# A second stage in an upper and a lower half: where the "y" products stand in a step

## The chip, the core and the metric

The kernel runs on one core of a Trainium2 chip. The metric is device time in microseconds (us): the median of three runs is 182.15 (181.86 to 182.22).

The core's engines have their own instruction streams and meet at semaphores: TensorE (PE, matrix products into the accumulator memory, PSUM, with its weight loads shown as PEld), VectorE (DVE), ScalarE (ACT), GpSimd (POOL) and SyncE (SP), which here issues the stores. PSUM has eight banks; a bank holds one result tile of 128 rows by 384 columns of float32 here.

## The reference, cut

Two layers. The first mixes each position with the six before it, with softmax weights per head. The second keeps 64 frequencies of the sequence, mixes channels in each of them, goes back, and ends in a product with `w_ch`:

```python
    x = attn_out
    X = np.fft.rfft(x, axis=1)
...
    y = np.fft.irfft(Y, n=S, axis=1)
    u = x + y
    return (u + np.maximum(u @ w_ch, 0.0)).astype(np.float32)
```

So the output is relu(x W + y W) + y + x. Since y comes from 64 frequencies, both y and y W are products with a table of 128 rows (64 cosines, 64 sines).

## The kernel before

All work up to some 108 us is untouched by the change: the input comes in, the seven-tap mixing runs as products with a band matrix (L270), the transform to 64 frequencies follows (L288), then the per-frequency channel products (L412), and the table of cosines and sines (`ftab`) and the mixed input (`ct`) are laid out for the last stage.

The last stage makes the output. The sequence is cut into 52 pairs of tiles (`duos`, 13 for each two batches), a tile being up to 128 positions of two batches. Pairs 0 to 3 are done by code of their own (`both`, `whole`, `full`). Pairs 4 to 51 give 96 items (`items`, one tile each, numbered from 0), and a loop over steps k (L628 to L663) works on several items at once. For each item, one PSUM bank collects:

- three products with W, 192 columns each, called c here (c0, c1, c2), and one of 384 columns, g, which adds y W;
- then ACT's `clamp` (L514), in place;
- then the product y (384 columns) on top of the clamped bank;
- then DVE's `add` (L501) of bank and x into one of seven output buffers. After the second tile of a pair SP issues the store (L509).

TensorE's array of 128 rows is used as two halves of 64. Each half has its own c0, c1, c2, g and y for an item: rows 0 to 63 ("lower") and rows 64 to 127 ("upper"). All are issued by `product` (L618). Both halves of an item write the same bank, and must not do so at the same time. So the upper half works on item k - 2 (`LAG = 2`) while the lower one works on item k, and where the upper half enters a bank that the lower one has written, `turn` makes the next weight load wait for that lower product. Program order within step k before the change:

1. a turn on the lower g of item k - 2, then c0, c1 of lower (item k) and upper (item k - 2) by turns;
2. lower y of item k - 4, which also waits for this item's clamp;
3. c2 and g of both halves, by turns, and the clamp of item k - 2;
4. a turn on the lower y just issued, then the upper y of item k - 4, and its add.

The last two items take y as one product over all 128 rows (`full`, L524).

The banks are handed out as a ring of eight (`next_of_ring`): an item takes the slot eight places after the earlier user, and its first lower product waits until that user's add is over. Six of the loop's steps also make `zw`, the weights of g and y for a batch to come (`WEIGHTS`: step to batch): two products over all rows (`zw_mm`, L479 and L480) into a ring slot of their own, and an ACT copy (`zw_out`, L487). Such a step hands out two slots. Batches 0 and 1 have their weights before the loop. Batches 2 and 3 are first used by pair 13 (step 18), batches 4 and 5 by pair 26 (step 44), 6 and 7 by pair 39 (step 70).

```python
    WEIGHTS = {2 * (n - FIRST): b for n, b in ((7, 2), (9, 3), (15, 4), (18, 5), (27, 6), (31, 7))}
```

The order of each engine is the order of the code: nothing is scheduled by a planner.

Of the kernel before, what the change touches and what calls it, by code (L numbers as in the profile page):

```python
# [19 lines left out]
def kernel(  # L20
# [418 lines left out]
    def z_pieces(u, row, which):  # L439
        r = slice(64 * row, 64 * row + 64)  # L440
        q, t = u
        if which == "c":
            b0, b1 = slice(0, D), slice(D, 2 * D)
            lhs = [ct[r, 3 * (NT * q + t) + w, :] for w in range(3)]
            if row == 0:
                return [(b0, lhs[0], wm[r, 0:D]), (b0, lhs[1], wsw[r, D:2 * D]), (b1, lhs[2], wsw[r, 0:D])]
            return [(b0, lhs[0], wm[r, 0:D]), (b1, lhs[1], wsw[r, 0:D]), (b1, lhs[2], w1[r, 0:D])]
        return [(slice(0, 2 * D), ftab[r, t, :],
                 zw[r, 0 if which == "g" else 1, 2 * q:2 * q + 2, :].rearrange("p b d -> p (b d)"))]
# [3 lines left out]
    def turn(names):  # L453
        nop = nc.tensor.nop()
        for name in names:
            tc.add_manual_dep(nop.ins, name, mybir.DependencyInfo(mybir.DependencyClass.Sync,
                                                                  mybir.DependencyReason.DATA),
                              reason="row tiles take turns on a bank")
# [19 lines left out]
    def zw_mm(b, bank):  # L478
        nc.tensor.matmul(bank[:, 0:2 * D], yet[:, 0, b, :], wm[:], start=True, stop=False)  # L479
        nc.tensor.matmul(bank[:, 0:2 * D], yet[:, 1, b, :], w1[:], start=False, stop=True)  # L480

    def zw_out(b, bank, on_scalar, t=None):
        ts = slice(0, 2) if t is None else slice(t, t + 1)
        dst = zw[:, ts, b, :]
        srcv = bank[:, 0:2 * D].rearrange("p (t d) -> p t d", t=2)[:, ts, :]
        if on_scalar:
            nc.scalar.activation(out=dst, in_=srcv, func=ACT.Copy, scale=ascale[:, 0:1])  # L487
        else:
            nc.vector.tensor_scalar(out=dst, in0=srcv, scalar1=ascale[:, 0:1], scalar2=None, op0=ALU.mult)
# [5 lines left out]
    def add(bank, n, a):  # L495

        o = outs[n % NO]
        q, t = duos[n][0]
        pn = PL if t == NT - 2 else P
        s = NT * q + t  # L500
        nc.vector.tensor_tensor(out=o[0:pn, :, a, :],  # L501
                                in0=bank[0:pn, 0:2 * D].rearrange("p (i d) -> p i d", i=2),
                                in1=xall[0:pn, s + a, :, :], op=ALU.add)
        apart = n in (0, N - 1)
        if apart or a == 1:
            a0, w = (a, 1) if apart else (0, 2)
            dst = bass.AP(tensor=out.tensor, offset=out.offset + (2 * q * S + P * t + a0) * D,
                          ap=[[2 * D, pn], [S * D, 2], [1, w * D]])
            nc.sync.dma_start(out=dst, in_=o[0:pn, :, a0:a0 + w, :].rearrange("p i a d -> p i (a d)"))  # L509

    def clamp(bank, on_scalar=True):
        z = bank[:, 0:2 * D]
        if on_scalar:
            nc.scalar.activation(out=z, in_=z, func=ACT.Relu)  # L514
        else:
            nc.vector.tensor_scalar(out=z, in0=z, scalar1=0.0, scalar2=None, op0=ALU.max)
# [5 lines left out]
    def full(n, which, a):  # L522
        (q, t), _ = duos[n]
        nc.tensor.matmul(place[n][a][:, 0:2 * D], ftab[:, t + a, :],  # L524
                         zw[:, 0 if which == "g" else 1, 2 * q:2 * q + 2, :].rearrange("p b d -> p (b d)"),
                         start=False, stop=(which == "y"), skip_group_check=True)
# [47 lines left out]
    def whole(n, which):  # L574
        for a in range(2):
            full(n, which, a)
# [23 lines left out]
    FIRST = 4  # L600
    LAG = 2
    items = [(n, a) for n in range(FIRST, N) for a in range(2)]
    K = len(items)
# [3 lines left out]
    def next_of_ring():  # L607
        if taken[0] == 4:
            ring.extend(z[:, 0, :] for z in open_psum("right", (1, 1, 1, 1)))
        taken[0] += 1  # L610
        return ring[(taken[0] - 1) % 8]

    bank = {}
    end = {}

    def product(k, row, piece, first, last):
        cols, l, r = piece
        mm = nc.tensor.matmul(bank[k][:, cols], l, r, start=first, stop=last, skip_group_check=True)  # L618
        end[k, row] = mm.ins.name

    def pieces(k, row, which):
        if not 0 <= k < K:
            return []
        n, a = items[k]
        return [p for w in which for p in z_pieces(duos[n][a], row, w)]

    WEIGHTS = {2 * (n - FIRST): b for n, b in ((7, 2), (9, 3), (15, 4), (18, 5), (27, 6), (31, 7))}
    for k in range(K + 4):  # L628
        if k in WEIGHTS:
            z = next_of_ring()  # L630
            zw_mm(WEIGHTS[k], z)
            zw_out(WEIGHTS[k], z, True)
        if k < K:
            bank[k] = next_of_ring()
            place.setdefault(items[k][0], []).append(bank[k])
        lower, upper = pieces(k, 0, "cg"), pieces(k - LAG, 1, "cg")
        mode0, mode1 = pieces(k - 4, 0, "y"), pieces(k - 4, 1, "y")
        if upper:
            turn([end[k - LAG, 0]])
        for j in range(4):  # L640
            if j == 2 and mode0:

                if k - 4 < K - 2:
                    product(k - 4, 0, mode0[0], False, False)
                else:
                    n, a = items[k - 4]
                    full(n, "y", a)
                    add(bank[k - 4], n, a)
            if lower:
                product(k, 0, lower[j], j == 0, False)  # L650
            if upper:
                product(k - LAG, 1, upper[j], False, False)
        if upper:
            clamp(bank[k - LAG])
        if k in (0, 2):
            n = 2 + k // 2
            whole(n, "y")
            for a in range(2):
                add(place[n][a], n, a)
        if mode1 and k - 4 < K - 2:  # L660
            turn([end[k - 4, 0]])
            product(k - 4, 1, mode1[0], False, True)
            add(bank[k - 4], *items[k - 4])  # L663
    for es in stacks.values():
        es.close()

# [29 lines left out]
```

## Time and profile before

| | |
|---|---|
| median of three runs | 182.15 us |
| profiled execution, its own time | 182.21 us |
| its span, first to last instruction | 180.4 us |
| PE busy in the span | 165.6 us (92%) |
| DVE busy | 121.3 us (67%) |
| ACT busy | 108.0 us (60%) |
| mean granted TensorE clock | 0.995 |
| L618 products, last stage, from | 112.6 us on |
| adds (L501) | 104, 556 ns each |
| clamps (L514) | 102, 475 ns each |
| stores of 384 KB | 47, median 3.2 us from issue to landing |

How to read rows: a row of a timeline has the start in us from the span's start, the duration in us, engine, line, operation, output and inputs, shape, and how many instructions in a row it merges (x3); in brackets the idle time of that engine just before, and what ended it. "64*128" is a product over 64 rows of the array. `z` is any PSUM bank, `arena` the output buffers, `mixa` holds `zw`. In a c product the second operand tells which it is: the lower half has wm, wsw, wsw; the upper half wm, wsw, w. A row of grouped instructions has the count, then busy us and mean ns of one, then the idle time before them. A row of stretches has busy us and count for PE, PEld, DVE, ACT, POOL, then granted clock, DMA share and GB/s. A row of DMA issues has count, size, and median us from issue to landing. A row of waits has us in total, times, and the longest.

### The profile page before, as it was taken

How to read it: one execution, taken by the hardware profiler on the slowest of the kernel's cores; microseconds unless marked ns; L12 is line 12 of the kernel's file. 1: busy time of each engine (PE TensorE's matmuls, PEld its weight loads, DVE VectorE, ACT ScalarE, POOL GpSimd, SP SyncE). 2: the span in 40 equal slices, each digit the busy share in tenths (PEclk: the TensorE clock that was granted, in tenths of full speed). 3: DMA queues.
4: the chain of work that ended last, by engine and by line, in shares of the span. 5: the costliest groups of instructions: out<-in, count | busy, mean ns of one | idle time of the engine just before them, and what ended most of it. 6: DMA issues, size and time to landing. Idle time of an engine off the chain costs nothing.

```text
span 180.4 us, 6521 instructions
## 1 busy us (share of the span) xinstructions
PE 165.6 (92%) x2765; PEld 129.8 (72%) x2765; DVE 121.3 (67%) x224; ACT 108.0 (60%) x193; POOL 49.1 (27%) x78
## 2 busy tenths in 40 slices
PE   7928999999999988999779989999999999999990
PEld 3617999999999967999667444567667667777760
DVE  5599894374354545787573005869789898999992
ACT  6327885434534425777563126487888787877870
POOL 7998743455322443444341000000000000000000
PEclk9999999999999999999999999999999999999998
DMA  2999999999999999999999920867779877898996
GB/s 34 162 192 192 191 194 192 191 191 192 196 189 196 208 206 207 206 206 207 208 205 207 189 35 0 297 260 294 270 272 337 337 260 279 335 337 306 331 341 225
DMA packets 50030, 40.04 MB, mean 222 GB/s; under 512 B 28305, under 2 KB 50001, under 8 KB 50001
## 3 DMA queue, kind: packets, MB, share of 16 engines
q0 software_dynamic: 35488, 19.54, 78.1%
q1 hardware_dynamic: 14512, 20.09, 30.3%
q8 instruction: 21, 0.34, 0.8%
q14 instruction: 9, 0.07, 0.1%
HBM read 39.10 MB, written 20.05 MB: 328 GB/s over the span
## 4 chain that ended last, share of the span: by engine, by line
DMA 49%; PE 39%; POOL 5%; issue 3%; DVE 0%; ACT 0%; DVEq 0%; POOLq 0%; ACTq 0%
PE z L618 33%; DMA xall<-in_x_dram 23%; DMA arena<-in_moe_w_i_dram 20%; DMA ct<-in_moe_w_i_dram 7%; POOL xall L142 5%; PE z L524 2%; PE z L479 1%; PE z L536 1%; PE z L473 1%; PE z L480 1%; PE z L412 1%; ACT ymix L421 0%; POOL arena L251 0%; DVE arena L501 0%; PE z L373 0%
## 5 line engine op out<-in xcount | busy, mean ns | idle before, releaser
L501 DVE TENSOR_TENSOR arena<-z,xall 128x384 f32<-128x384 f32 (+1 forms) x104 | 57.1, 556 | 8.8 <-PE z L618 4.5
L618 PE MATMUL z<-mixa,ftab 64*128 64x384 bf16 x380 | 58.0, 325 | 0.0
L514 ACT ACTIVATE z<-z 128x384 f32<-128x384 f32 x102 | 48.1, 475 | 13.8 <-PE z L618 3.0
L618 PE MATMUL z<-wsw,ct 64*128 64x192 bf16 x288 | 46.7, 243 | 0.0
L270 PE MATMUL z<-xall,band 128*64 128x192 bf16 (+3 forms) x832 | 38.8, 246 | 4.2 <-ACT band L193 3.3
L270 PEld LDWEIGHTS <-band 128*64 128x64 bf16 x832 | 36.6, 110 | 5.6 <-ACT band L193 3.6
L279 DVE CAST xall<-z 128x768 bf16<-128x768 f32 (+3 forms) x26 | 24.8, 956 | 20.5 <-PE z L270 18.4
L618 PE MATMUL z<-wm,ct 64*128 64x192 bf16 x192 | 38.3, 248 | 0.0
L618 PEld LDWEIGHTS <-ftab 64*128 64x128 bf16 x380 | 27.7, 94 | 14.4 <-PE z L618 11.2
L277 ACT CAST xall<-z 128x768 bf16<-128x768 f32 (+3 forms) x26 | 20.7, 796 | 19.4 <-PE z L270 19.1
L618 PEld LDWEIGHTS <-ct 64*128 64x128 bf16 x576 | 28.0, 94 | 3.1 <-issue 2.5
L142 POOL DMA_DIRECT2D xall<-in_x_dram x26 | 23.6, 914 | 12.8 <-DMA xall<-in_x_dram 12.1
L618 PE MATMUL z<-w,ct 64*128 64x192 bf16 x96 | 23.3, 243 | 0.0
L365 DVE COPY ct<-z 128x1024 bf16<-128x1024 bf16 x26 | 17.1, 686 | 7.3 <-PE z L373 4.9
L288 PE MATMUL z<-xall,ftab 128*64 128x384 bf16 (+1 forms) x208 | 21.0, 326 | 0.7 <-ACT xall L277 0.7
L373 PE MATMUL z<-ident,xall 128*128 128x128 bf16 x312 | 19.3, 219 | 0.2 <-ACT ftab L363 0.2
L373 PEld LDWEIGHTS <-xall 128*128 128x128 bf16 x312 | 17.7, 98 | 1.0 <-issue 0.3
L363 ACT COPY ct<-z 128x1024 bf16<-128x1024 bf16 x13 | 13.2, 1012 | 4.0 <-PE z L373 3.9
L288 PEld LDWEIGHTS <-ftab 128*64 128x64 bf16 (+1 forms) x208 | 13.6, 110 | 2.3 <-DVE xall L279 0.6
L251 POOL DMA_DIRECT2D arena<-in_moe_w_r_dram x13 | 8.0, 613 | 13.7 <-DMA xall<-in_x_dram 5.0
L421 ACT CAST ymix<-z 128x384 bf16<-128x384 f32 (+1 forms) x9 | 4.0, 443 | 12.4 <-PE z L412 12.2
L251 POOL DMA_DIRECT2D arena<-in_moe_w_i_dram x13 | 7.9, 610 | 12.4 <-DMA xall<-in_x_dram 5.5
(95 smaller groups left out, 128.4 us busy)
## 6 DMA issues: line engine op xcount, KB each, us to landing
out_dram<-arena SPq DMA_DIRECT2D x47, 384.0 KB, 3.2
xall<-in_x_dram POOLq DMA_DIRECT2D x14, 384.0 KB, 13.2
arena<-in_moe_w_r_dram POOLq DMA_DIRECT2D x13, 288.0 KB, 11.4
arena<-in_moe_w_i_dram POOLq DMA_DIRECT2D x13, 288.0 KB, 11.6
xall<-in_x_dram POOLq DMA_DIRECT2D x6, 432.0 KB, 13.4
ct<-in_moe_w_r_dram POOLq DMA_DIRECT2D x3, 288.0 KB, 11.5
ct<-in_moe_w_i_dram POOLq DMA_DIRECT2D x3, 288.0 KB, 11.5
out_dram<-arena SPq DMA_DIRECT2D x3, 288.0 KB, 3.4
```

The lines of the kernel that those rows point to most:

```text
L142: nc.gpsimd.dma_start(out=xall[:, s0:s0 + nf, i, :], in_=src)
L251: nc.gpsimd.dma_start(out=wts[g][64 * half:64 * half + 64, :, :, :], in_=src[4 * g:4 * g + 4, :, :].rearrange("m (p j) e -> p m j e", j=3))
L270: nc.tensor.matmul(o, lhs, xall[:, r0:r0 + 2 * n - 1:2, :, dsl], start=(main and a == 0), stop=not main, tile_position=(0, 64 * half), ski ...
L277: nc.scalar.copy(out=dst, in_=srcv)
L279: nc.vector.tensor_copy(out=dst, in_=srcv)
L288: nc.tensor.matmul(xp[r, :], ftab[0:k, t, r], xall[0:k, NT * q + t, :, :], start=(t == 0), stop=(t == NT - 1), tile_position=(0, 64 * hh), ...
L363: nc.scalar.copy(out=out, in_=in_)
L365: nc.vector.tensor_copy(out=out, in_=in_)
L373: nc.tensor.matmul(o, in_, ident[:], start=True, stop=True, is_transpose=True)
L501: nc.vector.tensor_tensor(out=o[0:pn, :, a, :], in0=bank[0:pn, 0:2 * D].rearrange("p (i d) -> p i d", i=2), in1=xall[0:pn, s + a, :, :], o ...
L514: nc.scalar.activation(out=z, in_=z, func=ACT.Relu)
L618: mm = nc.tensor.matmul(bank[k][:, cols], l, r, start=first, stop=last, skip_group_check=True)
```

## The change

Upper y of an item is issued one step later and in another place: not at the end of step k for item k - 4, but between the second and third c products of step k, for item k - 5. Lower y of item k - 4 moves behind the third c product, ahead of g. Their adds go with upper y. The pairs at which the weights of batches 2 to 7 are made move back, from 7, 9, 15, 18, 27, 31 to 9, 11, 17, 21, 28, 33, so the steps from 6, 10, 22, 28, 46, 54 to 10, 14, 26, 34, 48, 58.

Every product, load, clamp, add and store is still issued once. The turn before upper y now names a lower y of the step before. The turn at the start of each step, for the lower g of item k - 2, was covered by the turn of upper y in the step before and so asked for no wait of its own; in the changed program the first weight load of every step carries that wait.

```diff
-    WEIGHTS = {2 * (n - FIRST): b for n, b in ((7, 2), (9, 3), (15, 4), (18, 5), (27, 6), (31, 7))}
+    WEIGHTS = {2 * (n - FIRST): b for n, b in ((9, 2), (11, 3), (17, 4), (21, 5), (28, 6), (33, 7))}
+
+    def upper_y(k):
+        if 0 <= k < K - 2:
+            turn([end[k, 0]])
+            product(k, 1, pieces(k, 1, "y")[0], False, True)
+            add(bank[k], *items[k])
+
+    def lower_y(k):
+        if 0 <= k < K - 2:
+            product(k, 0, pieces(k, 0, "y")[0], False, False)
+        elif K - 2 <= k < K:
+            n, a = items[k]
+            full(n, "y", a)
+            add(bank[k], n, a)
+
     for k in range(K + 4):
...
         lower, upper = pieces(k, 0, "cg"), pieces(k - LAG, 1, "cg")
-        mode0, mode1 = pieces(k - 4, 0, "y"), pieces(k - 4, 1, "y")
         if upper:
             turn([end[k - LAG, 0]])
         for j in range(4):
-            if j == 2 and mode0:
-
-                if k - 4 < K - 2:
-                    product(k - 4, 0, mode0[0], False, False)
-                else:
-                    n, a = items[k - 4]
-                    full(n, "y", a)
-                    add(bank[k - 4], n, a)
+            if j == 2:
+                upper_y(k - 5)
+            if j == 3:
+                lower_y(k - 4)
             if lower:
                 product(k, 0, lower[j], j == 0, False)
             if upper:
                 product(k - LAG, 1, upper[j], False, False)
...
-        if mode1 and k - 4 < K - 2:
-            turn([end[k - 4, 0]])
-            product(k - 4, 1, mode1[0], False, True)
-            add(bank[k - 4], *items[k - 4])
```

## Prediction, made before the changed kernel was run

> **What bounds the kernel now.** I read first the chain of waits (shares by engine, then by line), then busy time by stretches of the last stage, where all of the change lies.
>
> ```profile
> PE z L618 33%; DMA xall<-in_x_dram 23%; DMA arena<-in_moe_w_i_dram 20%; DMA ct<-in_moe_w_i_dram 7%; POOL xall L142 5%; PE z L524 2%; PE z L479 1%; PE z L536 1%; PE z L473 1%; PE z L480 1%; PE z L412 1%; ACT ymix L421 0%; POOL arena L251 0%; DVE arena L501 0%; PE z L373 0%
> ...
> 120.00:140.00 20.00, 20.00 (x318) 14.07 (x318) 16.81 (x31) 16.18 (x34) 0.00 (x0) 1.00 0.79 292
> 140.00:160.00 20.00, 20.00 (x324) 14.29 (x320) 17.51 (x33) 16.08 (x34) 0.00 (x0) 1.00 0.84 310
> 160.00:175.00 15.00, 15.00 (x249) 10.94 (x244) 14.09 (x26) 12.05 (x26) 0.00 (x0) 1.00 0.90 326
> ```
>
> From 112 us on TensorE's products (L618) carry the chain; PE is never idle, its clock is 1.00, DVE has 6% to 16% to spare, ACT 20%. But the DMA share climbs to 0.90, so the second thing to watch is the stores. Busy PE does not say that both halves of the array work, so I took one step apart (PE, then its weight loads).
>
> ```profile
> 140.31 0.51 PE L618 MATMUL z<-mixa,ftab 64*128 64x384 bf16 x3
> 140.49 0.25 PE L618 MATMUL z<-wm,ct 64*128 64x192 bf16 x1
> 140.58 0.24 PE L618 MATMUL z<-wsw,ct 64*128 64x192 bf16 x1
> 140.66 0.24 PE L618 MATMUL z<-wm,ct 64*128 64x192 bf16 x1
> 140.66 0.32 PE L618 MATMUL z<-mixa,ftab 64*128 64x384 bf16 x1
> 140.74 0.24 PE L618 MATMUL z<-wsw,ct 64*128 64x192 bf16 x1
> 140.82 0.24 PE L618 MATMUL z<-w,ct 64*128 64x192 bf16 x1
> 140.82 0.24 PE L618 MATMUL z<-wsw,ct 64*128 64x192 bf16 x1
> 140.90 0.51 PE L618 MATMUL z<-mixa,ftab 64*128 64x384 bf16 x3
> 141.08 0.25 PE L618 MATMUL z<-wm,ct 64*128 64x192 bf16 x1
> ...
> 141.07 0.09 PEld L618 LDWEIGHTS <-ftab 64*128 64x128 bf16 x1 [0.15 <-PE z L618]
> ...
> PEld L618 <- PE z L618: 11.2, 74, 0.2
> ...
> 140.68 0.47 ACT L514 ACTIVATE z<-z 128x384 f32<-128x384 f32 x1
> L514 ACT ACTIVATE z<-z 128x384 f32<-128x384 f32 x28 | 13.3, 475 | 3.3
> ```
>
> The lower rows do c0 (140.49), c1 (140.58), y (140.66), c2 (140.82, wsw), g (140.90); the upper rows y (third of the three at 140.31, from 140.48), c0 (140.66), c1, c2 (140.82, w), g. Both chains are gapless; the upper one runs a y behind. The last row covers 28 clamps from 157.4 us, one per step: (13.3 + 3.3)/28 = 0.593 us a step. Of that, three products of 192 columns take 0.0825 each (140.66 to 140.74 to 140.82) and two of 384 take 0.1625 each (140.66 to 140.82): 0.5725. The missing 0.021 is at the weight load of upper y: it waits for lower y of the same step (0.15 idle, in 74 steps) and is therefore not done ahead, nor is that of lower c0 behind it. Both products then start 0.010 late and run 0.010 longer (0.25 against 0.24).
>
> **Part 1: upper y a step later, behind c1; lower y behind c2.** Counts of products, loads, adds and stores are unchanged. What matters is when the waits are over.
>
> ```profile
> 115.17 0.33 PE L618 MATMUL z<-mixa,ftab 64*128 64x384 bf16 x2
> 115.17 0.10 PEld L618 LDWEIGHTS <-ct 64*128 64x128 bf16 x2
> ...
> 117.35 0.32 PE L618 MATMUL z<-mixa,ftab 64*128 64x384 bf16 x1
> 117.73 0.09 PEld L618 LDWEIGHTS <-ftab 64*128 64x128 bf16 x1
> ```
>
> The turn now asks for a lower y of the step before. After a weights step the upper rows were free and the load came when only the turn held it: lower y of 117.35 ends at 117.67, the load starts at 117.73, so a turn costs 0.057 behind the end. In the new order lower y starts 0.2475 into a step, ends at 0.57, releases at 0.627; the load of upper y wants to go with upper c1, at 0.5725 + 0.0825 = 0.655. That is early by 0.028. A satisfied wait is free: the pair of loads at 115.17 holds the first one of step 4, which waits for a product of step 2, and still it goes with the g products before it. The new order also gives lower c0 such a wait in each step (for the g of two steps before, over by a step). Bounds for the 0.021: gone, or kept in full; I take gone. Gain 93 x 0.021 = 1.95 us.
>
> Lower y also waits for its clamp: now 1.39 us after the step of its g began, against a clamp done at 0.41 (g) + 0.32 + 0.05 (140.63 to 140.68) + 0.475 + 0.05 = 1.31: 0.08 to spare, where it had 0.04 (0.35 + 0.593 from g to y today, against 0.90).
>
> **Part 2: the weights steps.** These rows are the weights products and what stands around them.
>
> ```profile
> 142.68 0.51 PE L618 MATMUL z<-mixa,ftab 64*128 64x384 bf16 x3
> 143.12 0.34 PE L479 MATMUL z<-wm,yet 128*128 128x384 bf16 x1
> 143.30 0.33 PE L480 MATMUL z<-w,yet 128*128 128x384 bf16 x1
> 143.55 0.26 PE L618 MATMUL z<-wm,ct 64*128 64x192 bf16 x2
> ...
> 144.48 0.55 DVE L501 TENSOR_TENSOR arena<-z,xall 96x384 f32<-96x384 f32 x1 [0.70 <-PE z L618]
> ```
>
> Today upper y runs alone ahead of them (from 142.86), and afterwards the upper rows wait out the same y: the add is 0.70 - 0.04 = 0.66 late, six times. In the new order both halves end together with g: 0.26 + 0.18 + 0.25 = 0.69 from g to the next c0 in place of 0.16, so 0.53. Gain 6 x 0.13 = 0.8. Where in the loop these steps stand does not change their cost on PE; weights are ready by far (batch 3 in step 14, first used in step 18).
>
> **Part 3: the ring of eight banks.** Upper y, and with it the add, come 0.165 later. From upper y to a free bank:
>
> ```profile
> 140.85 0.56 DVE L501 TENSOR_TENSOR arena<-z,xall 128x384 f32<-128x384 f32 x1
> ...
> 111.91 2.88 DVE L501 TENSOR_TENSOR arena<-z,xall 128x384 f32<-128x384 f32 x6 [0.89 <-PE z L524]
> ...
> 107.74 0.22 DVE L435 COPY yet<-z 128x64 bf16<-128x64 bf16 x1 [2.99 <-PE z L373]
> 108.02 0.34 PE L479 MATMUL z<-wm,yet 128*128 128x384 bf16 x1 [0.26 <-DVE yet L435]
> ```
>
> 0.32 (product) + 0.04 (140.82 to 140.85) + 0.557 + 0.05 (107.96 to 108.02) = 0.97, so the bank is free 1.14 after the start of that step. DVE keeps up: adds can follow by (2.88 - 0.55)/5 = 0.47. With all banks in the ring an item needs a bank three steps later: covered. With one slot held by weights it is two steps, 1.145 against 1.14: at the edge, 26 items, each 0 to 0.02; I take 0.3, and 0.2 more for upper rows that then lag before five weights steps. With two weights among the last eight slots (steps 10 and 14) item 15 takes the bank of item 9, whose upper y is now in step 14: lower c0 of step 15, and all of PE behind it, waits 1.14 - 0.57 = 0.57. Item 14 has 0.03. Today item 11 takes that of item 5, whose upper y runs ahead of the weights: covered. Loss 0.3 + 0.2 + 0.6 = 1.1.
>
> Row "x94" below holds the adds from the first item's to the third from last: 52.2 + 7.8, less the first idle 0.38 and the last add 0.56, is 59.1 us. New: 59.1 - 1.95 - 0.8 + 1.1 = 57.5. The first add comes 0.08 later (upper y 0 a step on), the last adds 0.07 (c2 and g of the last step are all that lies between two upper y). DVE ends 1.6 - 0.15 = 1.4 us earlier.
>
> ```profile
> L501 DVE TENSOR_TENSOR arena<-z,xall 128x384 f32<-128x384 f32 (+1 forms) x94 | 52.2, 557 | 7.8 <-PE z L618 4.5
> ...
> 157.06 0.37 SPq L509 DMA_DIRECT2D out_dram<-arena  x1
> out_dram<-arena SPq DMA_DIRECT2D x1, 384.0 KB, 2.6
> ...
> 167.68 0.37 SPq L509 DMA_DIRECT2D out_dram<-arena  x1
> q8 instruction: 1, 0.02, 9.5%
> out_dram<-arena SPq DMA_DIRECT2D x1, 384.0 KB, 4.2
> ...
> 175.99 0.37 SPq L509 DMA_DIRECT2D out_dram<-arena  x1
> out_dram<-arena SPq DMA_DIRECT2D x1, 384.0 KB, 2.7
> SPq L691 <- DMA out_dram<-arena: 1.6, 3, 0.9
> ```
>
> **Part 4: the stores give half of it back.** The program ends when SP has seen the last stores land. A store issued at 157.06 landed in 2.6 us, about the least; the one of 167.68, beside an instruction load that held one of 16 DMA engines for 9.5% of 16 x 1.1 = 1.7 us, in 4.2; seven stores on, 2.7. So a queue stands, and shrinks by 0.22 a store: issued every 1.19, served every 0.97. New interval 2 x 0.5725 = 1.145: it shrinks by 0.175, and the 16 stores from 157 us on end 16 x 0.042 = 0.7 us further behind. Of 1.4 there arrive 0.65 to 0.7 (bounds: 0.4 and 1.4). Sum against the profiled execution (182.21 us, 1.8 of it outside its span of 180.4): 182.2 - 0.65 = 181.55; the median shown is 0.06 less than that execution: 181.5.
>
> **Rivals.** (1) The turn still comes too late, since 0.028 us is all it is early by. Then the step stays at 0.593; gains are the weights steps' 0.8 less the stall of 0.6: 182.0. For it: modelled ends; against: the free wait at 115.17.
>
> (2) The stores give nothing back: the queue drains between instruction loads, as it had by 157.06. Then 182.2 - 1.4 = 180.8. Against: the 0.90 share at the end.
>
> (3) The ring costs more, the slower side: with one slot lent to weights, each lower c0 waits for an add that a later upper y has set back. If an add frees its bank 0.15 late instead of 0.05, two steps of 1.145 do not suffice by 0.1, and 26 items lose some 0.05 each, 1.3 us, the tight pair 0.1 more: PE's gain is gone, the stores end behind as now, about 182.7. It decides from 0.12 on. Against: 0.05 at 108.02.
>
> (4) The two halves do not pass each other. In strict program order lower y would wait for upper c2, this for upper y: 0.0825 x 2 + 0.1625 x 3 = 0.6525 a step, 93 x 0.059 = 5.5 us more, 187.6. Against: today's order would take 0.6525 as well, and takes 0.593; at 140.58 lower c1 starts ahead of upper c0 (140.66), which stands before it in the program. The Trainium skill ("TensorE: Matmul & The Clock Gate", Part 3) states just this order: "MATMULs are pc-monotone in start AND end — strict FIFO, no reordering". By it the step would take those 0.6525 us; the trace does not agree.
>
> **How the numbers follow.** Forecast 56%, by its own range 181.1 to 181.9 (gains from 0.35 to 1.05); rivals 16%, 10%, 16%, 2%. A difference under 0.2% (0.36 us) cannot be told from none here. Faster: 48 of the 56, and rival 2: 58%. Same: the other 8, and rival 1: 24%. Slower: rivals 3 and 4: 18%. The range from 180.7 to 182.5 takes in rivals 1 and 2 and leaves out 3 and 4.
>
> **What will show it.** Right: clamps 0.573 apart; no 0.15 idle before weight loads; c0 of both halves starting together; one gap of some 0.6 on PE shortly after the second weights step; last add about 1.4 us earlier, its store landing 3 us or more after issue. Wrong: clamps 0.593 apart (turn), PE waiting for DVE in many steps (ring), stores that land in 2.5 at the end.

## The result, and the profile after

The changed kernel takes 180.56 us (median of seven runs, 180.16 to 181.53) against 182.15; the ratio is 0.992, with a 95% interval of 0.990 to 0.995. So it is faster, by 1.6 us, where 0.65 had been forecast, and the median lies 0.14 us under the low end of the stated range. The execution that was profiled is the slowest of the seven (181.53 us, span 179.8). All ratios and medians are of fast executions; of the profiles used below only that of the old order with half stores is of a slow one (185.0 us at a granted clock of 0.979), and it is read in the last stage alone, where its clock is 1.00 like that of the others.

Busy time by stretches of the last stage, changed kernel (the columns are as before):

```profile
120.00:140.00 20.00, 19.60 (x318) 15.86 (x315) 16.99 (x31) 16.10 (x35) 0.00 (x0) 1.00 0.78 286
140.00:160.00 20.00, 20.00 (x337) 17.03 (x335) 18.21 (x34) 16.63 (x36) 0.00 (x0) 1.00 0.88 323
160.00:174.00 14.00, 14.00 (x230) 12.03 (x226) 13.63 (x26) 11.67 (x25) 0.00 (x0) 1.00 0.93 341
```

PE is as "busy" as it was, but in the second stretch it ran 337 products where it had run 324. (The busy time of weight loads rose by more, from 14.3 to 17.0 us. It does not count them: loads that run at the same time count once, and 320 loads of 0.094 us were busy for 14.3.) In the first one 0.40 us is missing on PE, a gap that was not there before. DVE is at 97% and the DMA share at 0.93 at the end.

One step, by the timeline of PE and then of its weight loads:

```profile
160.45 0.32 PE L618 MATMUL z<-mixa,ftab 64*128 64x384 bf16 x1
...
160.77 0.26 PE L618 MATMUL z<-wm,ct 64*128 64x192 bf16 x2
160.86 0.33 PE L618 MATMUL z<-wsw,ct 64*128 64x192 bf16 x3
160.96 0.39 PE L618 MATMUL z<-mixa,ftab 64*128 64x384 bf16 x2
161.12 0.24 PE L618 MATMUL z<-w,ct 64*128 64x192 bf16 x1
161.18 0.34 PE L618 MATMUL z<-mixa,ftab 64*128 64x384 bf16 x2
161.35 0.24 PE L618 MATMUL z<-wm,ct 64*128 64x192 bf16 x1
```

```profile
160.88 0.09 PEld L618 LDWEIGHTS <-ftab 64*128 64x128 bf16 x1
160.88 0.09 PEld L618 LDWEIGHTS <-ct 64*128 64x128 bf16 x1
```

Both halves begin with c0 (two at 160.77, 0.02 apart) and end with g (two at 161.18). The first row is the lower y of the step before; it ends at 160.77. The load of upper y, which waits for it, goes at 160.88 (the `ftab` one), with no idle time before it. And so for the whole stage, in the rows of waits and of grouped instructions (clamps of 27 steps; adds from the first item's to the third from last):

```profile
PEld L618 <- PE z L618: 2.1, 7, 0.3
```

```profile
L514 ACT ACTIVATE z<-z 128x384 f32<-128x384 f32 x27 | 12.8, 475 | 2.6
...
L501 DVE TENSOR_TENSOR arena<-z,xall 128x384 f32<-128x384 f32 (+1 forms) x94 | 52.1, 557 | 6.3 <-PE z L618 4.6
```

Waits of weight loads for PE fell from 74 to 7. A step takes (12.8 + 2.6)/27 = 0.570 by rounded terms; single adds follow each other by 0.572 to 0.573. The stretch of adds is 52.1 + 6.3 - 0.46 (idle before the first) - 0.56 = 57.4 us, where it was 59.1.

The two places where the new order pays, on PE, and on DVE behind it:

```profile
122.69 0.34 PE L618 MATMUL z<-mixa,ftab 64*128 64x384 bf16 x2
123.43 0.26 PE L618 MATMUL z<-wm,ct 64*128 64x192 bf16 x2 [0.40 <-DVE arena L501]
...
149.69 0.34 PE L618 MATMUL z<-mixa,ftab 64*128 64x384 bf16 x2
149.97 0.34 PE L479 MATMUL z<-wm,yet 128*128 128x384 bf16 x1
150.14 0.33 PE L480 MATMUL z<-w,yet 128*128 128x384 bf16 x1
150.40 0.26 PE L618 MATMUL z<-wm,ct 64*128 64x192 bf16 x2
```

```profile
122.82 0.56 DVE L501 TENSOR_TENSOR arena<-z,xall 128x384 f32<-128x384 f32 x1 [0.59 <-PE z L618]
123.97 1.13 DVE L501 TENSOR_TENSOR arena<-z,xall 128x384 f32<-128x384 f32 x2 [0.59 <-PE z L618]
...
150.94 0.56 DVE L501 TENSOR_TENSOR arena<-z,xall 128x384 f32<-128x384 f32 x1 [0.55 <-PE z L618]
```

At 123.43, one step after the second weights step, c0 waits for an add (that of 122.82 ends at 123.38, so 0.05 before): the 0.40 is PE fully idle, and the adds show two late ones in a row, the weights step (122.82) and this wait (123.97). A later weights step runs g at 149.69, weights products at 149.97 and 150.14, c0 at 150.40. The add behind it is late by 0.55 - 0.02 = 0.53, no longer 0.66.

The stores at the end, each in a row of issues (count, size, us to landing); the last row is the program's last store:

```profile
out_dram<-arena SPq DMA_DIRECT2D x1, 384.0 KB, 4.9
...
out_dram<-arena SPq DMA_DIRECT2D x1, 384.0 KB, 3.6
out_dram<-arena SPq DMA_DIRECT2D x1, 144.0 KB, 3.4
```

They were issued at 165.34, 174.44 and 175.44. In this execution the queue stood at 4.9 us, and had shrunk only to 3.4 at the end; before the change the last store took 2.5. The last add ended 1.56 us earlier than before (175.33 against 176.89), the last store landed 0.66 earlier (178.81 against 179.47): 0.9 us was given back.

### The profile page after: what moved, and what is told of

Read it like the earlier page. It is cut to its first block, busy times and chain, and to the rows that moved or that the text cites. A ratio compares the mean times of both kernels' runs of the same rounds, so it can differ in the third digit from the quotient of the medians.

```text
span 179.8 us, 6519 instructions
## 1 busy us (share of the span) xinstructions
PE 164.7 (92%) x2765; PEld 136.4 (76%) x2765; DVE 120.1 (67%) x224; ACT 107.8 (60%) x193; POOL 49.5 (28%) x78
## 4 chain that ended last, share of the span: by engine, by line
DMA 50%; PE 38%; POOL 5%; issue 3%; DVE 1%; ACT 0%; DVEq 0%; POOLq 0%; ACTq 0%
PE z L618 32%; DMA xall<-in_x_dram 23%; DMA arena<-in_moe_w_i_dram 20%; DMA ct<-in_moe_w_i_dram 7%; POOL xall L142 5%; PE z L524 2%; PE z L479 1%; PE z L536 1%; PE z L473 1%; PE z L480 1%; DVE arena L501 1%; PE z L412 1%; ACT ymix L421 0%; POOL arena L251 0%; PE z L373 0%
## 5 line engine op out<-in xcount | busy, mean ns | idle before, releaser
L618 PE MATMUL z<-mixa,ftab 64*128 64x384 bf16 x380 | 54.9, 323 | 0.0
L618 PEld LDWEIGHTS <-ct 64*128 64x128 bf16 x576 | 36.3, 94 | 8.5 <-PE z L618 1.9
L618 PE MATMUL z<-wsw,ct 64*128 64x192 bf16 x288 | 32.2, 242 | 0.0
L618 PEld LDWEIGHTS <-ftab 64*128 64x128 bf16 x380 | 31.0, 94 | 0.8 <-PE z L618 0.2
L618 PE MATMUL z<-wm,ct 64*128 64x192 bf16 x192 | 25.9, 244 | 0.4 <-DVE arena L501 0.4
```

## Experiments

Seven kernels ran, in two groups, each group on a chip of its own, with the kernel before on the same chip. Ratios are to that. What is compared first is the stretch of adds, since it lies inside the last stage: the first add of the loop comes anywhere between 116.3 and 117.9 us in all profiles but one (119.0), which moves whole runs by as much as the change does. The chips differ too: the kernel before took 182.69 and 182.67 us on these two, against 182.15 on the chip of the first runs, so where a time was expected, its ratio tells more.

### The order alone

The changed kernel, with the old weights steps:

```diff
-    WEIGHTS = {2 * (n - FIRST): b for n, b in ((9, 2), (11, 3), (17, 4), (21, 5), (28, 6), (33, 7))}
+    WEIGHTS = {2 * (n - FIRST): b for n, b in ((7, 2), (9, 3), (15, 4), (18, 5), (27, 6), (31, 7))}
```

> The changed order of the y products with the old weights steps (6, 10, 22, 28, 46, 54). Theory (the gain is the order's): step 0.573 us, add of the first item to add of the third from last 57.4 to 57.6 us as in the changed kernel, and one stall of about 0.57 on PE, now at item 11 (steps 6 and 10 are as close as 10 and 14). Time 180.3 to 181.2, like the changed kernel. Rival (the old places of the weights steps do harm in the new order): stalls in more steps, 58 us or more, time over 181.5.

Measured: ratio 0.994 (0.992 to 0.997). Its group of adds, and the adds around the stall:

```profile
L501 DVE TENSOR_TENSOR arena<-z,xall 128x384 f32<-128x384 f32 (+1 forms) x94 | 52.1, 557 | 6.3 <-PE z L618 4.6
```

```profile
120.79 0.56 DVE L501 TENSOR_TENSOR arena<-z,xall 128x384 f32<-128x384 f32 x1 [0.59 <-PE z L618]
121.94 1.13 DVE L501 TENSOR_TENSOR arena<-z,xall 128x384 f32<-128x384 f32 x2 [0.60 <-PE z L618]
```

57.4 us again, and the same two late adds in a row, now four steps sooner. The gain on PE is the order's; the move of the weights steps neither adds to it nor takes from it. The time of 181.7 us is above the expected 180.3 to 181.2, but on this chip the kernel before took 182.69: 1.0 us of gain.

### The weights steps alone

The kernel before, with the new weights steps (the reverse of the edit above).

> The old order of the y products with the new weights steps (10, 14, 26, 34, 48, 58). Theory: step 0.593 us, each weights step still 0.66 us longer, no stall for a bank, 59.1 us from the first item's add to the third from last, time as before, 182.0 to 182.3. Rival (the later weights steps bring the gain): time 181.3 or less.

Measured: ratio 1.002 (0.999 to 1.005); 182.93 us, above the expected 182.0 to 182.3, and 0.2 above the kernel before on the same chip.

```profile
L501 DVE TENSOR_TENSOR arena<-z,xall 128x384 f32<-128x384 f32 (+1 forms) x94 | 52.3, 558 | 7.8 <-PE z L618 4.5
```

52.3 + 7.8 - 0.37 - 0.56 = 59.2 us, as before the change; from add to add five of the six weights steps cost 1.254 to 1.256 us, and one 1.185, behind an add that was 0.07 late. So the rival that the later weights bring the gain is out.

### Weights steps eight apart

```diff
-    WEIGHTS = {2 * (n - FIRST): b for n, b in ((9, 2), (11, 3), (17, 4), (21, 5), (28, 6), (33, 7))}
+    WEIGHTS = {2 * (n - FIRST): b for n, b in ((7, 2), (11, 3), (17, 4), (21, 5), (28, 6), (33, 7))}
```

> The changed kernel with batch 2's weights made at pair 7 in place of 9, so that the first two weights steps are 6 and 14, eight steps apart, and no item takes a bank that was freed only six places back. Theory: the stall of 0.57 us at item 15 is gone, the stretch from first to third last add goes from 57.4 to 56.8 us, and DVE ends 0.6 us earlier; of this the stores let through between nothing and all: time 0 to 0.6 us under the changed kernel's. Rival (that gap is not the ring's): the gap stays, 57.4 us.

Measured: ratio 0.990 (0.986 to 0.994), the lowest of the kernels that store all of their output.

```profile
L501 DVE TENSOR_TENSOR arena<-z,xall 128x384 f32<-128x384 f32 (+1 forms) x94 | 52.1, 558 | 5.7 <-PE z L618 3.9
```

```profile
119.69 4.02 DVE L501 TENSOR_TENSOR arena<-z,xall 128x384 f32<-128x384 f32 x7
124.26 2.92 DVE L501 TENSOR_TENSOR arena<-z,xall 128x384 f32<-128x384 f32 x5 [0.55 <-PE z L618]
```

The stretch is 52.1 + 5.7 - 0.46 - 0.56 = 56.8, 0.6 us shorter (by the starts of the adds 56.86 against 57.41); after the second weights step (124.26) five adds follow without a break, where the changed kernel has one late by 0.59. The gap is the ring's. In time, the interval of this kernel overlaps that of the changed one, so that it is ahead of that one is shown on the adds and not in the runs.

### The turn asked sooner

Upper y stands one c product earlier; everything else as in the changed kernel.

```diff
-            if j == 2:
+            if j == 1:
                 upper_y(k - 5)
```

> The changed kernel with upper y one c product earlier (between c0 and c1). The halves still end each step together; only the turn is asked 0.08 us sooner, when the lower y of the step before, by 0.627 us after its step began against a load due at 0.575, is not yet released. Theory (a late turn costs 0.021 us a step): step 0.593 us, first to third last add 58.6 to 59.0 us, 0.15 idle before weight loads again, time 181.7 to 182.2. Rival (the gain comes from both halves ending together, wherever upper y stands): step 0.573, time as the changed kernel.

Measured: ratio 0.997 (0.995 to 1.000); the 182.35 us are above the expected 181.7 to 182.2 and 0.3 below the kernel before on this chip. Weight loads, waits, and adds:

```profile
160.36 0.09 PEld L618 LDWEIGHTS <-ftab 64*128 64x128 bf16 x1 [0.15 <-PE z L618]
160.96 0.09 PEld L618 LDWEIGHTS <-ftab 64*128 64x128 bf16 x1 [0.15 <-PE z L618]
```

```profile
PEld L618 <- PE z L618: 10.9, 65, 0.3
```

```profile
L501 DVE TENSOR_TENSOR arena<-z,xall 128x384 f32<-128x384 f32 (+1 forms) x94 | 52.3, 558 | 7.4 <-PE z L618 4.4
```

The idle 0.15 is back, in 65 steps, 0.59 us apart, and the stretch is 52.3 + 7.4 - 0.46 - 0.56 = 58.7 us. Both halves still end a step together here: the weights steps keep the low cost (1.112 to 1.114 us from add to add in five of six, over a step of 0.592, so 0.52). So the two gains are separate. That a turn is answered in time is worth 58.7 - 57.4 = 1.3 us, net of what else changes with it; the shared end is worth the 0.13 of a weights step and no more.

### Half stores, in both orders

Each store writes only the first half of a tile's positions, so half of the output is left out.

```diff
-                          ap=[[2 * D, pn], [S * D, 2], [1, w * D]])
-            nc.sync.dma_start(out=dst, in_=o[0:pn, :, a0:a0 + w, :].rearrange("p i a d -> p i (a d)"))
+                          ap=[[2 * D, pn // 2], [S * D, 2], [1, w * D]])
+            nc.sync.dma_start(out=dst, in_=o[0:pn // 2, :, a0:a0 + w, :].rearrange("p i a d -> p i (a d)"))
```

The new order:

> The changed kernel, storing only the first half of the positions of each tile (the other half of the output is left out), so that each store is half as long and no queue can stand. Theory (PE's gain of some 1.6 us reaches the end of the adds, and the queue of stores then decides how much of it arrives): adds unchanged (57.4 us from the first item's to the third from last), the last store lands about 2.0 to 2.2 us after its issue, and the time is 1.4 to 1.7 us under that of the old order with half stores. Rival (stores also hold up the adds, by buffers or by traffic): the stretch of the adds gets shorter than 57.3 us.

The old order:

> The kernel before, storing only the first half of the positions of each tile (the other half of the output is left out). Theory: the stretch of the adds stays at 59.1 us, the last store lands 2.0 to 2.2 us after its issue in place of 2.5, so the time falls by 0.3 to 0.5 us to 181.7 to 181.9 on the chip of the first runs; the difference to the changed kernel with half stores is PE's gain alone, 1.4 to 1.7 us. Rival (the stores bound the kernel before): the time falls by more than 1 us.

Measured: ratios 0.990 (0.987 to 0.994) and 1.001 (0.997 to 1.004). The medians differ by 182.64 - 180.65 = 2.0 us, over the expected 1.4 to 1.7, but with intervals of about 0.6 us on either side. Adds, new order, then old:

```profile
L501 DVE TENSOR_TENSOR arena<-z,xall 128x384 f32<-128x384 f32 (+1 forms) x94 | 52.1, 558 | 6.3 <-PE z L618 4.6
```

```profile
L501 DVE TENSOR_TENSOR arena<-z,xall 128x384 f32<-128x384 f32 (+1 forms) x94 | 52.3, 558 | 7.8 <-PE z L618 4.5
```

57.4 and 59.2, as with full stores: the stores do not hold up the adds in either order. Nor did the old order get faster, as had been expected by 0.3 to 0.5 us. A half store alone landed no sooner (median 2.7 us, where full ones land in 2.4 when nothing stands before them). The last store, a smaller one, did land 2.16 and 2.20 us after its issue, as expected, but SP issued it 0.4 us after the last add in place of 0.1. So these runs do not show what a kernel without a queue would take. They do show that with half the load the end is the same in both orders: the last store lands 2.60 us after the last add in the new order and 2.63 in the old.

### The changed kernel once more

> The changed kernel unaltered, on the chip of the two runs with half stores, to see how much the end of the stores differs between executions of one program. Theory (instruction loads and stores meet differently each time): stretch of the adds again 57.4 us to within 0.1, but the last store's time from issue to landing anywhere from 2.4 to 3.4 us (3.4 in the first profile). Rival (the order fixes it): 3.3 to 3.5 again.

Measured: ratio 0.993 (0.991 to 0.996).

```profile
L501 DVE TENSOR_TENSOR arena<-z,xall 128x384 f32<-128x384 f32 (+1 forms) x94 | 52.1, 558 | 6.3 <-PE z L618 4.6
```

```profile
out_dram<-arena SPq DMA_DIRECT2D x1, 144.0 KB, 2.7
```

The adds are as they were; the last store lands in 2.7 us, not 3.4. From the last add to the last landing, by profile:

| | full stores | last add to last landing, us |
|---|---|---|
| old order | before; weights alone | 2.58; 2.45 |
| new order | after; again; order alone; eight apart | 3.48; 2.80; 2.70; 2.78 |
| upper y early (0.59 step) | | 2.53 |

With the shorter step the end of the stores comes 0.2 to 0.3 us later than the mean of the old order's two in three profiles of four, and nearly 1.0 in the fourth. The order does not fix it. The instruction loads do meet the stores at other places from profile to profile (the last two start at 159.31 and 167.47 us in the first profile of the changed kernel, at 160.71 and 168.57 in this one), but that they are the cause of the spread is not shown.

## Why the prediction was right, and where its size was off

**The step.** The bound was read rightly: a turn answered too late, twice 0.010 us in each step. The gain came as forecast, and the load now goes at 160.88 with upper c1. "The turn asked sooner" moved only the due time, to before the release, and lost the 0.021 a step again. Rival 1 is out for the changed kernel, and is what that experiment shows.

The margin of 0.028 was not there, though. It rests on a turn that costs 0.057 us behind the product's end, read at one place. In the step above lower y ends at 160.77 and the load starts at 160.88, 0.11 later; in the old order it is 0.09 (lower y of 140.66 ends at 140.98, the load is at 141.07). In the trace of the changed kernel the load of upper y comes 0.041 or 0.042 us after an update of the turn's semaphore in 76 of 94 steps; in the old order, where the load plainly waited, it comes 0.042 or 0.043 after one in all 94. So most often the release still seems to be what lets the load go. In the step shown it starts 0.005 us after upper c1, where loads that wait for nothing start 0.001 or 0.002 after theirs, and its product is not late for it. The wait was over just in time: that it cost nothing was partly luck.

**Passing.** Rival 4 is out: the step is 0.573, not 0.6525.

**The weights steps.** Forecast 0.13 each; measured 1.256 - 0.593 = 0.66 before and 1.110 - 0.573 = 0.54 after, so 0.13, in the last three. The first three gave less: they cost 0.63, 0.58 and 0.61, of which the third got 0.07 back with the next add.

**The ring.** The place and size of the one wait were right (forecast 0.57 behind item 14's weights step; 1.152 - 0.573 = 0.58). All of the ring's loss was put at 1.1 us. By the sum it is 57.4 less the 59.1 - 1.95 - 0.8 = 56.4 without it: 1.0, of which the tight pair has 0.6 (shown by moving it). The rest, 0.4, is a difference that no run isolates; in the trace it sits in the first weights steps, as above, and in adds some 0.06 late a few steps behind later ones. That these are the "edge" cases of the ring is not shown. Rival 3, at 0.15 us from add to bank, is out: at 123.43 it was 0.05, and PE waited for DVE that one time.

**The adds' end.** Forecast 57.5, measured 57.4. The first add came 0.08 later against the one before it, as worked out; the expected 0.07 at the last adds did not come (from the third from last on they end after 1.48 us, where it was 1.49). DVE's end: forecast 1.4 earlier, measured 1.56 on the clock and 59.15 - 57.41 - 0.08 = 1.66 against the start of the loop.

**The stores: the step that was mis-sized.** "Of 1.4 there arrive 0.65 to 0.7": the queue was said to take 0.7 back. It took back 0.9 in the first profile after, which thus came out at the forecast 181.5, but this is the slowest of seven runs; in the three other profiles of the 0.573 step with full stores it took 0.2 to 0.3, and the last store landed in 2.6 to 2.7 us, close to the 2.5 that had been named as a sign of being wrong. The working carried one profile's queue, with its instruction loads, over to a new order. (The 2.6 us of its first store were not quite the least either: such stores land in 2.4.) The measured 1.6 us (1.0 to 1.9 by the interval) lie above the bounds of 0.4 and 1.4 that were given for what arrives; on another chip, in "The changed kernel once more", the same kernel gained 1.2. That the runs without a profile had the short tail is an inference: their time before the last stage is not on record either. Rival 2 (nothing given back, 180.8) was nearer to the time, though not right in all of its mechanism: some is given back, and PE's gain was larger by 0.2 to 0.3.

## What to carry to other kernels

In this kernel a semaphore wait on a weight load was free when it ended as the product ahead began on that half, and cost 0.02 us a step when it was asked one product, 0.08 us, sooner; what lies between was not run. Count back from the release and place the load behind that point, with some room: from the end of a product to a load that waited for it this case has 0.06, 0.09 and 0.11 us at different places. A producer moved later in a step also frees its buffer later: look at the steps in which the ring lends a slot to something else, and keep such steps apart. With eight banks and the new order, two of them four steps apart cost 0.58 us in both places that were tried; eight apart cost no such wait, nor did the six between steps 22 and 28 in "The order alone". Where the tail is a queue of transfers, take its length from several profiles before it goes into a sum.

## What the runs showed of the hardware beside this

A store of half the rows did not land sooner: 2.7 us at the median against 2.4 for an unhindered full one, though 192 KB against 384. Two stores of 192 KB over all 128 rows, at the start of the last stage, landed in 2.0 us in each profile with full stores; the runs do not show why. And weights products over all 128 rows cost time for going in and out: from g at 149.69 to them 0.28, between them 0.17, and from the second to the next c0 0.26, where g to c0 takes 0.16 otherwise. That is some 0.12 to go in and 0.09 to come out, beside 0.34 for the two products.
